# Staging copies and DMA transposes for the remainder channels of octs -1 and 0, a remainder term summed once for the two steps of a pair, and SPREAD 12, in a dilated convolution on one NeuronCore

## The chip, the cores and the metric

One core of one Trainium2 chip. The metric is the device time of one execution in microseconds (us). Runs of one kernel agree within 1%. A ratio is the mean time of one kernel's runs over that of the other's runs in the same rounds on the same chip, so it is not quite the ratio of the medians that stand beside it; its interval is a 95% interval. PE is the matrix engine, ACT the scalar engine, DVE the vector engine; SP issues the transfers.

## The reference

A causal convolution of 15 taps with dilation 2 over 16,000 steps of 144 channels, batch 2, into 288 channels; then a gate and a projection.

```python
B, T, D, K = (2, 16000, 144, 15)
xp = jnp.pad(x, ((0, 0), (28, 0), (0, 0)))
h = sum(jnp.einsum('btc,cd->btd', xp[:, 28 - 2*i : 28 - 2*i + T, :], w[i]) for i in range(K))
z = jnp.tanh(h[..., :D]) * sigmoid(h[..., D:])
return z @ w_o
```

(The loop of the reference is written as a sum here.)

## The kernel before

The time axis is cut into segments of 8 steps, "octs". A step has 144 channels, which do not fit 128 rows, so the first 128 lie transposed in `XA` and the 16 that remain are packed, several steps together, into `XBc`, and lie transposed in `XB`. The convolution runs in difference form: sums of weights (`WS`, `WC`, `WT`, `WV`, `WD`) on PE meet differences of inputs (`V`, `DU`, `DD`, `GX` to `GD`) made by DVE. The work before steady state is: octs -1 and 0 direct, as one "direct" pair and pairs 0 to 3, then "units" of two octs each, which repeat to the end. XA(3) stands for the `XA` of oct 3, and so on. `Xr` is a chunk of the input as loaded, `ZT` is `Z` transposed, `WOR` holds the weights of the projection, and a bank is one of the parts of PSUM in which PE sums.

A program in Python orders all operations by estimated times before anything runs; on the chip, each engine goes through its own list in order. So one edit can move operations far away from it. `soft` and `SPREAD` are hints to that ordering: `SPREAD` sets how early in a unit the differences of the next are put into DVE's list.

How octs -1 and 0 get their `XB` in the old kernel: 12 PE transposes into PSUM and two evictions by ACT.

```python
for o, tiles, bb in ((-1, range(E0 - 4, E0), 7), (0, range(E0, E0 + 8), 6)):
    ...
    g.add("pe", fns, r=hk5 + ["XBcz", "ID"], alloc=[bk], dur=0.06 * len(fns))
    xb_op = g.add("act", lambda v, ...: v.activation(XB[:, bslot(o), i0:8, :]..., PSb[:, ...], ACT.Copy), ...)
```

All later octs go through a staging copy `STB` (ACT or DVE) and a DMA transpose issued by SP; `XA` goes through `STA` likewise:

```python
def load_xb(o, parts=(0, 1)):
    ...
    for h in parts:
        ...   # STB[:, q, 6h:6h+6, :] <- XBc, one copy of 768 columns for each half
    return g.add("sp", lambda e: e.dma_start_transpose(XB[:, s, :, :], STB[:, q, :, :]...), ...)
```

The end of a pair adds its remainders, two matmuls for each of its two steps, and then ACT does tanh and sigmoid (`finish`) and DVE multiplies them into `Z`:

```python
def pair_end(q):
    k0 = k_of(q)
    direct_b(k0, _Half(dp[q + 1], 0))
    direct_b(k0 + 2, _Half(dp[q + 1], 1))
    return finish(dp[q + 1], zdir(k0), zdir(k0 + 2))
```

In a unit, the three combining sums of DVE (`Xp <- PS, UX`), then `PS <- PS, UX` and `PS <- PS, Xp`, give back or fill PSUM banks on which PE's next blocks (`WA,DD` and `WA,GD`) start.

Of the kernel before, what the change touches and what calls it, by code (L numbers as in the profile page):

```python
# [5 lines left out]
ACT = mybir.ActivationFunctionType  # L6
# [5 lines left out]
NP = 128  # L12
# [315 lines left out]
def _conv_wavenet_kernel(nc, x, w, w_o, out):  # L328
# [44 lines left out]
    EARLYC = 0  # L373
    NQ0 = 2
    NQD = 0
    SPREAD = 10
    SPREAS = 9
    PATTERN = "Y0a O2+ X0a+ O1+ Y0b X0b+ D11 D00 S0+ X1a+ D10 Y01 S1+ X1b+ D01 VE+ VF+ O0+"

    with contextlib.ExitStack() as st:  # L380
# [73 lines left out]
        def bslot(o):  # L454
            return (o + 1) % NB

        def oct_of(e):
            return (e - E0) // 8, (e - E0) % 8
# [5 lines left out]
        def xb_tile(e):  # L464
            o, i = oct_of(e)
            return XB[:, bslot(o), i, :]

        def win_b(e):
            c4, m4 = (e + 2) % 4, (e + 2) // 4
            return XBc[:, 4 + c4, MB - 1 - m4:MB - 1 - m4 + 8, :].rearrange("p m c -> p (m c)")  # L470
# [140 lines left out]
        g.add("pool", fix, r=xp_keys[2], w=hk, dur=0.3)  # L611
        for o, tiles, bb in ((-1, range(E0 - 4, E0), 7), (0, range(E0, E0 + 8), 6)):
            fns = []
            for e in tiles:
                c0 = bb * 1024 + 128 * oct_of(e)[1]
                fns.append(lambda t, e_=e, c=c0: t.transpose(PSb[:, c:c + 128], win_b(e_), ID[:]))
            bk = _Bank(bb)
            g.add("pe", fns, r=hk5 + ["XBcz", "ID"], alloc=[bk], dur=0.06 * len(fns))
            i0 = oct_of(tiles[0])[1]
            xb_op = g.add("act", lambda v, o=o, i0=i0, bb=bb: v.activation(XB[:, bslot(o), i0:8, :].rearrange("p a b -> p (a b)"), PSb[:, bb * 1024 + 128 * i0:bb * 1024 + 1024], ACT.Copy),  # L620
                  r=[bk], w=[("XB", bslot(o))], frees=[bk], dur=0.5 if o < 0 else 0.92)


        wak = [("WA", i) for i in range(4)]
# [40 lines left out]
        def load_xb(o, parts=(0, 1)):  # L665
            s, q = bslot(o), o % NST
            e0 = E0 + 8 * o
            ck = set()
            for e in range(e0 - 28, e0 + 8):
                if e >= EP:  # L670
                    ck.update([("XBc", chunk_of(e - E0)), ("XBd", chunk_of(e - E0))])
                else:
                    ck.update(hk5 + ["XBcz", "XBd_h"])
            m4 = (e0 + 2) // 4

            for h in parts:
                def cp(v, h=h):
                    src = bass.AP(XBc[:].tensor, (MB - 1 - m4 - h) * DB, [[8 * MB * DB, NP], [MB * DB, 6], [1, 128]])
                    dst = STB[:, q, 6 * h:6 * h + 6, :]
                    return v.tensor_copy(dst, src) if o in BDVE else v.activation(dst, src, ACT.Copy)  # L680
                g.add("dve" if o in BDVE else "act", cp, r=sorted(ck, key=str), w=[("STB", q, h)], dur=0.27 if o in BDVE else 0.708, prio=2 if gate else 0, soft=gate[:1])
            if 1 not in parts:
                return
            return g.add("sp", lambda e: e.dma_start_transpose(XB[:, s, :, :], STB[:, q, :, :].rearrange("p a b -> p (a b)")),
                  r=[("STB", q, 0), ("STB", q, 1)], w=[("XB", s)], dur=1.7, dma="xb", nbytes=12 * 128 * 128 * 2)

# [389 lines left out]

        def direct_b(k, b):
            e = H + k
            g.add("pe", region(b, [lambda: xb_tile(e), lambda: xb_tile(e - 2)], [lambda: WB[:, 0, :], lambda: WB[:, 1, :]]),
                  r=[("XB", bslot(-1)), ("XB", bslot(0)), ("WB", 0), ("WB", 1)], w=[b.bk], floating=k >= KF, prio=2 if k >= KF else 1, dur=2 * MM)  # L1080


        if ("r", 0) not in LOADS:
            load_xchunk(0).deps.add(wa_op)
# [13 lines left out]
        QS = [(0, 0), (0, 1), (1, 0), (1, 1)]  # L1098

        def jset(pi):  # L1100
            return [2 * pi, 2 * pi + 1]

        def pair_sum(q, pi, after=None):
            n, r = QS[q]
            bk = dp[q + 1]
            es = [E0 + 4 * n + r - 4 * j for j in jset(pi)]
            pre = [mm(_Half(bk, 1), lambda: ID[:], lambda: WA[:, 12, :], True)] if q == 2 and pi == 3 else []
            g.add("pe", pre + region(_Half(bk, 0), [(lambda e=e: xa_tile(e)) for e in es], [(lambda j=j: WS[:, j, :] if j < 7 else WA[:, 14, :]) for j in jset(pi)], pi == 3),
                  r=[("XA", aslot(oct_of(e)[0])) for e in es] + [("WS", pi), ("WA", pi)], dur=(2 + len(pre)) * MM, floating=True, prio=2, soft=(after,), **({"alloc": [bk]} if pi == 3 else {"w": [bk]}))
            if pi == 0:  # L1110
                g.add("act", lambda e: e.activation(bank(bk.b + 1), bank(bk.b), ACT.Copy), w=[bk], dur=t_act(N2), prio=0)  # L1111
# [13 lines left out]

        def k_of(q):
            return 2 + 4 * QS[q][0] + QS[q][1]

        def pair_end(q):
            k0 = k_of(q)  # L1130
            direct_b(k0, _Half(dp[q + 1], 0))
            direct_b(k0 + 2, _Half(dp[q + 1], 1))
            return finish(dp[q + 1], zdir(k0), zdir(k0 + 2))

        for pi, (t0, t1) in wa_order:
            for k in range(2):
                direct(k, db[k], pi, t0, t1)
            for q in range(NQ0):
                if q < NQD:
                    for i in range(2):  # L1140
                        direct(k_of(q) + 2 * i, _Half(dp[q + 1], i), pi, t0, t1)
                else:
                    pair_sum(q, pi, xb_op if q == 2 and pi == 3 else None)
        for k in range(2):
            direct_b(k, db[k])
        fin = finish(dp[0], zdir(0), zdir(1))
        for q in range(4):
            if q >= NQ0:
                for pi in range(3, -1, -1):
                    pair_sum(q, pi, (xb_op if q == 2 else fin) if pi == 3 else None)  # L1150
            for pi in range(3, -1, -1):
                if q >= NQD:
                    pair_own(q, pi)
            pair_end(q)
        load_xa(1)
        compact_chunk(0)
        g.add("act", lambda a: a.activation(WC[:, 2, 3, :], WB[:, 1, :], ACT.Copy, scale=-1.0), r=[("WB", 1)], w=[("WB", 3)], dur=0.31, prio=2)
        diff_b("dve", 3, 7, hk5 + ["XBcz"], "XBd_h")
        diff_chunk(0)
# [3 lines left out]
        for i in range(4):  # L1163
# [3 lines left out]
            else:  # L1167
                wsum(lambda: WC[:, 1, 3, :], lambda: WA[:, 12, :], lambda: WA[:, 14, :], [("WA", 3)], [("WC", 1, 3)], 0.25)
                wsum(lambda: WC[:, 0, 3, :], lambda: WC[:, 1, 3, :], lambda: WA[:, 13, :], [("WC", 1, 3), ("WA", 3)], [("WC", 0, 3)], 0.25)
        wsum(lambda: WB[:, 2, :], lambda: WB[:, 0, :], lambda: WB[:, 1, :], [("WB", 0), ("WB", 1)], [("WB", 2)], 0.25)  # L1170
        wsum(lambda: WT[:, 0:2, :], lambda: bass.AP(WC[:].tensor, 0, [[12 * N2, NP], [2 * N2, 2], [1, N2]]), lambda: bass.AP(WC[:].tensor, N2, [[12 * N2, NP], [2 * N2, 2], [1, N2]]),
# [205 lines left out]
```

## Time and profile before

| | before |
|---|---|
| median of 3 runs | 321.79 us (321.76 to 321.99) |
| profiled execution | 321.02 us, span 319.0 us, granted clock full in every stretch used here |
| matmuls | 2643 |
| busy: PE, DVE, ACT, POOL | 97%, 89%, 84%, 5% |
| DMA share of 16 engines, from 10 to 45 us | 82.6% for the hardware queue |

The prediction below shows the lines and how to read them.

### The profile page before, as it was taken

The numbers are of one execution on the slowest core, as the hardware profiler recorded it, in microseconds if no ns is written. First come the engines' busy times: TensorE is split into PE (matmuls) and PEld (weight loads), VectorE is DVE, ScalarE is ACT, GpSimd is POOL, SyncE is SP. The second block draws the span as 40 slices with busy tenths as digits, with TensorE's granted clock in tenths as the row PEclk, the third lists the DMA queues.
The fourth block names the chain that finished last, engine by engine and source line by source line (L and its number), as shares of the span: only waits on it lengthen the run. The fifth ranks groups of instructions, "written<-read, shape, count | busy, mean of one in ns | idle before, by whom it ended". The sixth has DMA issues, their size and how long they took to land.

```text
span 319.0 us, 6912 instructions
## 1 busy us (share of the span) xinstructions
PE 310.7 (97%) x2643; PEld 239.1 (75%) x2643; DVE 284.6 (89%) x615; ACT 267.5 (84%) x635; POOL 16.6 (5%) x29
## 2 busy tenths in 40 slices
PE   7999999999999999999999999999999999999994
PEld 6677667777777777777777777777777777777673
DVE  2999999999999998999989999898989989894774
ACT  3896699898897989989798897979889797788674
POOL 8106400000000000000000000000000000000000
PEclk9999999999999999999999999999999999999999
DMA  8699969949987592988949495894949477131553
GB/s 206 209 207 165 266 117 218 179 128 183 194 165 197 105 245 73 209 165 122 251 92 238 94 205 156 147 210 108 229 111 183 100 131 184 46 69 74 113 131 92
DMA packets 127821, 50.38 MB, mean 158 GB/s; under 512 B 119134, under 2 KB 121615, under 8 KB 127789
## 3 DMA queue, kind: packets, MB, share of 16 engines
q1 hardware_dynamic: 127273, 49.62, 74.1%
q0 software_dynamic: 512, 0.33, 0.4%
q8 instruction: 20, 0.33, 0.4%
q14 instruction: 12, 0.10, 0.1%
q10 hardware_dynamic: 4, 0.01, 0.0%
HBM read 11.82 MB, written 9.22 MB: 66 GB/s over the span
## 4 chain that ended last, share of the span: by engine, by line
PE 86%; ACT 7%; DMA 4%; SPq 1%; issue 1%; DVE 0%; ACTq 0%
PE PS L747 76%; PE PS L846 9%; DMA XA<-STA 2%; ACT STB L680 2%; DMA Xp<-in_x_dram 2%; ACT STA L659 1%; ACT TS L768 1%; SPq L479 1%; ACT TS L771 1%; ACT PS L905 1%; ACT XB L620 0%; SPq L491 0%; PE PS L579 0%; PE PS L877 0%; ACT XA L588 0%
## 5 line engine op out<-in xcount | busy, mean ns | idle before, releaser
L1026 DVE TENSOR_TENSOR Xp<-PS,UX 128x576 f32<-128x576 f32 x90 | 63.0, 751 | 16.7 <-PE PS L747 16.6
L747 PE MATMUL PS<-WB,XB 128*128 128x288 bf16 x260 | 72.1, 286 | 0.0
L1038 DVE TENSOR_TENSOR PS<-PS,Xp 128x576 f32<-128x576 f32 x90 | 68.4, 760 | 2.1 <-ACT OS L854 1.0
L747 PE MATMUL PS<-WA,GD 128*128 128x288 bf16 x360 | 70.0, 286 | 0.1
L768 ACT ACTIVATE TS<-PS 128x288 f16<-128x288 f32 x125 | 51.7, 413 | 13.3 <-PE PS L747 12.3
L854 ACT ACTIVATE OS<-PS 128x432 bf16<-128x432 f32 (+1 forms) x88 | 42.3, 489 | 14.0 <-PE PS L846 12.8
L771 ACT ACTIVATE TS<-PS 128x288 f16<-128x288 f32 x125 | 51.4, 411 | 0.0
L905 ACT ACTIVATE PS<-PS 128x288 f32<-128x288 f32 x120 | 46.3, 408 | 2.8 <-PE PS L747 2.8
L974 ACT ACTIVATE UX<-PS 128x576 f32<-128x576 f32 x60 | 39.2, 654 | 10.7 <-PE PS L747 10.4
L680 ACT ACTIVATE STB<-XBc 128x768 bf16<-128x768 bf16 x56 | 47.5, 854 | 0.0
L747 PE MATMUL PS<-WS,GU 128*128 128x288 bf16 x210 | 44.3, 287 | 0.0
L846 PE MATMUL PS<-WOR,ZT 128*128 128x144 bf16 (+1 forms) x322 | 42.4, 253 | 0.2 <-DVE Xp L1026 0.2
L747 PEld LDWEIGHTS PS<-WA,GD 128*128 128x128 bf16 x360 | 33.7, 98 | 11.4 <-DVE PS L1038 3.2
L776 DVE TENSOR_TENSOR Z<-TS 128x288 bf16<-128x288 f16 x125 | 36.9, 301 | 4.4 <-ACT TS L771 4.2
L747 PE MATMUL PS<-WC,XB 128*128 128x288 bf16 x120 | 34.3, 286 | 0.0
L846 PEld LDWEIGHTS PS<-WOR,ZT 128*128 128x128 bf16 x322 | 27.9, 98 | 6.6 <-ACT OS L854 0.5
L747 PE MATMUL PS<-WD,DD 128*128 128x288 bf16 x180 | 31.9, 286 | 0.2 <-ACT PS L905 0.2
L747 PE MATMUL PS<-WC,V 128*128 128x288 bf16 x180 | 30.6, 286 | 0.0
L747 PE MATMUL PS<-WA,DD 128*128 128x288 bf16 x180 | 30.6, 286 | 0.0
L747 PEld LDWEIGHTS PS<-WB,XB 128*128 128x128 bf16 x260 | 25.4, 98 | 6.7 <-ACT XB L620 0.3
L747 PE MATMUL PS<-WA,V 128*128 128x288 bf16 x118 | 25.7, 286 | 0.3 <-ACT PS L1111 0.3
L747 PE MATMUL PS<-WT,DU 128*128 128x288 bf16 x120 | 24.5, 286 | 0.0
(93 smaller groups left out, 459.4 us busy)
## 6 DMA issues: line engine op xcount, KB each, us to landing
Xr<-in_x_dram SPq DMA_DIRECT2D x15, 576.0 KB, 4.6
out_dram<-OS SPq DMA_DIRECT2D x30, 288.0 KB, 3.0
WA<-in_w_dram SPq DMA_DIRECT2D x3, 288.0 KB, 5.3
ZT<-Z SPq DMA_TRANSPOSE x32, 3.7
Xp<-in_x_dram SPq DMA_DIRECT2D x2, 252.0 KB, 5.4
XA<-STA SPq DMA_TRANSPOSE x30, 3.5
XB<-STB SPq DMA_TRANSPOSE x30, 4.4
Xp<-in_x_dram SPq DMA_DIRECT2D x1, 441.0 KB, 4.1
```

The lines of the kernel that those rows point to most:

```text
L479: return e.dma_start(tile_ap, src)
L680: return v.tensor_copy(dst, src) if o in BDVE else v.activation(dst, src, ACT.Copy)
L747: return lambda t: t.matmul(bank(bk.b), lhsT=lhs(), rhs=rhs(), start=start, stop=True, skip_group_check=True)
L768: return a.activation(TS[:, s, 0, :, :], both(bk, 0, D), ACT.Tanh)
L771: return a.activation(TS[:, s, 1, :, :], both(bk, D, D), ACT.Sigmoid)
L776: return v.tensor_tensor(dst, TS[:, s, 0, :, :], TS[:, s, 1, :, :], ALU.mult)
L846: return t.matmul(PS[:, c0:c0 + n * D], lhsT=ZT[:, zt, blk, :], rhs=WOR[:, wi:wi + n, :].rearrange("p a b -> p (a b)"), start=first, stop= ...
L854: return e.tensor_copy(dst, src) if eng == "dve" else e.activation(dst, src, ACT.Copy)
L905: g.add("act", lambda e: e.activation(bank(bk.b + 1), bank(bk.b), ACT.Copy), w=[bk], dur=t_act(N2), prio=0)
L974: g.add("act", lambda e: e.activation(UX[:, k, u % NU, :, :], both(X, 0, N2), ACT.Copy), r=[X], w=[("UX", k, u % NU)], frees=[X], dur=t_ac ...
L1026: g.add("dve", lambda v, k=k, wi=wi, vb=vb, us=us: v.tensor_tensor(wslot(wi), both(vb, 0, N2), UX[:, k, us, :, :], ALU.add), r=[vb, ("UX", ...
L1038: return v.tensor_tensor(both(d, 0, N2), src, wslot(wi), ALU.add)
```

## The change

It sends octs -1 and 0 the way of all the others: `STB`, then a DMA transpose, of 4 blocks for oct -1 and 12 for oct 0. With this the remainders of these octs are in difference form, so a term with the weights `WB0 + WB1` is common to the two steps of a pair. In pairs 2 and 3 (`SHX`) it is summed once, ahead of the copy from one bank to the other. `SPREAD` goes from 10 to 12.

```diff
+    SHX = (2, 3)
-    SPREAD = 10
+    SPREAD = 12
...
-        for o, tiles, bb in ((-1, range(E0 - 4, E0), 7), (0, range(E0, E0 + 8), 6)):
-            ... 12 PE transposes, 2 ACT evictions ...
...
+                    p0 = 2 if o < 0 else 0
+                    src = bass.AP(XBc[:].tensor, (p0 * MB + MB - 1 - m4 - h) * DB, ...)
+                    dst = STB[:, q, 6 * h + p0:6 * h + 6, :]
...
+            b0 = 8 if o < 0 else 0
+            return g.add("sp", lambda e: e.dma_start_transpose(XB[:, s, b0:12, :], STB[:, q, b0:12, :]...), ...)
...
-            region(b, [lambda: xb_tile(e), lambda: xb_tile(e - 2)], [WB0, WB1])
+            out = [(XB tile of the own difference, WB0 or -WB1)]
+            if shared_too: out.append((XB tile of the shared step, WB0 + WB1))
...
+        diff_b("dve", 1, 9, hk5 + ["XBcz"], "XBd_h")
+        load_xb(-1, (1,))
+        load_xb(0)
...
+            if pi == 0 and q in SHX:
+                tw, keys = rem(k_of(q))
+                g.add("pe", region(_Half(bk, 0), [tw[1][0]], [tw[1][1]]), ...)
...
-            direct_b(k0, _Half(dp[q + 1], 0))
-            direct_b(k0 + 2, _Half(dp[q + 1], 1))
+            direct_b(k0, _Half(dp[q + 1], 0), q not in SHX)
+            direct_b(k0 + 2, _Half(dp[q + 1], 1), q not in SHX)
...
-                    pair_sum(q, pi, xb_op if q == 2 and pi == 3 else None)
+                    pair_sum(q, pi, None)
```

(Weights and tiles are named in words where the code is long.)

More of the change, by code (lines that the diff above doesn't have):

```diff
@@ L611, in _conv_wavenet_kernel @@
         g.add("pool", fix, r=xp_keys[2], w=hk, dur=0.3)
-        for o, tiles, bb in ((-1, range(E0 - 4, E0), 7), (0, range(E0, E0 + 8), 6)):
-            fns = []
-            for e in tiles:
-                c0 = bb * 1024 + 128 * oct_of(e)[1]
-                fns.append(lambda t, e_=e, c=c0: t.transpose(PSb[:, c:c + 128], win_b(e_), ID[:]))
-            bk = _Bank(bb)
-            g.add("pe", fns, r=hk5 + ["XBcz", "ID"], alloc=[bk], dur=0.06 * len(fns))
-            i0 = oct_of(tiles[0])[1]
-            xb_op = g.add("act", lambda v, o=o, i0=i0, bb=bb: v.activation(XB[:, bslot(o), i0:8, :].rearrange("p a b -> p (a b)"), PSb[:, bb * 1024 + 128 * i0:bb * 1024 + 1024], ACT.Copy),
-                  r=[bk], w=[("XB", bslot(o))], frees=[bk], dur=0.5 if o < 0 else 0.92)
         wak = [("WA", i) for i in range(4)]
@@ L672, in load_xb @@
                 else:
-                    ck.update(hk5 + ["XBcz", "XBd_h"])
+                    ck.update(hk5 + ["XBcz", "XBd_h", "XBd0"])
             m4 = (e0 + 2) // 4
@@ L677, in cp @@
                 def cp(v, h=h):
-                    src = bass.AP(XBc[:].tensor, (MB - 1 - m4 - h) * DB, [[8 * MB * DB, NP], [MB * DB, 6], [1, 128]])
-                    dst = STB[:, q, 6 * h:6 * h + 6, :]
+                    p0 = 2 if o < 0 else 0
+                    src = bass.AP(XBc[:].tensor, (p0 * MB + MB - 1 - m4 - h) * DB, [[8 * MB * DB, NP], [MB * DB, 6 - p0], [1, 128]])
+                    dst = STB[:, q, 6 * h + p0:6 * h + 6, :]
                     return v.tensor_copy(dst, src) if o in BDVE else v.activation(dst, src, ACT.Copy)
@@ L683, in load_xb @@
                 return
-            return g.add("sp", lambda e: e.dma_start_transpose(XB[:, s, :, :], STB[:, q, :, :].rearrange("p a b -> p (a b)")),
-                  r=[("STB", q, 0), ("STB", q, 1)], w=[("XB", s)], dur=1.7, dma="xb", nbytes=12 * 128 * 128 * 2)
+            b0 = 8 if o < 0 else 0
+            return g.add("sp", lambda e: e.dma_start_transpose(XB[:, s, b0:12, :], STB[:, q, b0:12, :].rearrange("p a b -> p (a b)")),
+                  r=[("STB", q, 1)] + ([("STB", q, 0)] if o >= 0 else []), w=[("XB", s)], dur=1.7, dma="xb", nbytes=(12 - b0) * 128 * 128 * 2)
         def xbk(o):
@@ L1075, in direct, with rem, direct_b @@
                   r=[("XA", aslot(o)) for o in sorted(set(oct_of(e - DIL * i)[0] for i in range(t0, t1)))] + [("WA", pi)], dur=(t1 - t0) * MM, floating=k >= KF, prio=2 if k >= KF else 1, soft=(after,), **({"alloc": [b.bk]} if t0 == 12 and b.i == 0 else {"w": [b.bk]}))
-        def direct_b(k, b):
-            e = H + k
-            g.add("pe", region(b, [lambda: xb_tile(e), lambda: xb_tile(e - 2)], [lambda: WB[:, 0, :], lambda: WB[:, 1, :]]),
-                  r=[("XB", bslot(-1)), ("XB", bslot(0)), ("WB", 0), ("WB", 1)], w=[b.bk], floating=k >= KF, prio=2 if k >= KF else 1, dur=2 * MM)
+        def rem(k, shared_too=True):
+            o, dl = (-1, 6 + k) if k < 2 else (0, k - 2)
+            r, p = dl % 2, 3 - dl // 2
+            kk, j = p // 2, p % 2
+            bb = 6 * (1 - kk)
+            out = [(lambda: XB[:, bslot(o), bb + (2 if j == 0 else 0) + r, :], (lambda: WB[:, 0, :]) if j == 0 else (lambda: WC[:, 2, 3, :]))]
+            if shared_too:
+                out.append((lambda: XB[:, bslot(o), bb + 4 + r, :], lambda: WB[:, 2, :]))
+            return out, [("XB", bslot(o)), ("WB", 0 if j == 0 else 3), ("WB", 2)]
+        def direct_b(k, b, shared_too=True):
+            tw, keys = rem(k, shared_too)
+            g.add("pe", region(b, [x[0] for x in tw], [x[1] for x in tw]), r=keys, w=[b.bk], floating=k >= KF, prio=2 if k >= KF else 1, dur=len(tw) * MM)
+        g.add("act", lambda a: a.activation(WC[:, 2, 3, :], WB[:, 1, :], ACT.Copy, scale=-1.0), r=[("WB", 1)], w=[("WB", 3)], dur=0.31, prio=2)
+        g.add("pool", lambda p: p.tensor_copy(XBc[:, 2:4, MB - 1, :], XBc[:, 6:8, MB - 1, :]), r=hk5 + ["XBcz"], w=["XBd0"], dur=0.3)
+        diff_b("dve", 1, 9, hk5 + ["XBcz"], "XBd_h")
+        load_xb(-1, (1,))
+        load_xb(0)
+        wsum(lambda: WB[:, 2, :], lambda: WB[:, 0, :], lambda: WB[:, 1, :], [("WB", 0), ("WB", 1)], [("WB", 2)], 0.25)
         if ("r", 0) not in LOADS:
@@ L1098, in _conv_wavenet_kernel, with k_of @@
         QS = [(0, 0), (0, 1), (1, 0), (1, 1)]
+        def k_of(q):
+            return 2 + 4 * QS[q][0] + QS[q][1]
         def jset(pi):
@@ L1109, in pair_sum @@
                   r=[("XA", aslot(oct_of(e)[0])) for e in es] + [("WS", pi), ("WA", pi)], dur=(2 + len(pre)) * MM, floating=True, prio=2, soft=(after,), **({"alloc": [bk]} if pi == 3 else {"w": [bk]}))
+            if pi == 0 and q in SHX:
+                tw, keys = rem(k_of(q))
+                g.add("pe", region(_Half(bk, 0), [tw[1][0]], [tw[1][1]]), r=keys, w=[bk], dur=MM, floating=True, prio=2)
             if pi == 0:
@@ L1124, in pair_own @@
             g.add("pe", fns, r=keys, w=[bk], dur=len(fns) * MM, floating=True, prio=2)
-        def k_of(q):
-            return 2 + 4 * QS[q][0] + QS[q][1]
         def pair_end(q):
             k0 = k_of(q)
-            direct_b(k0, _Half(dp[q + 1], 0))
-            direct_b(k0 + 2, _Half(dp[q + 1], 1))
+            direct_b(k0, _Half(dp[q + 1], 0), q not in SHX)
+            direct_b(k0 + 2, _Half(dp[q + 1], 1), q not in SHX)
             return finish(dp[q + 1], zdir(k0), zdir(k0 + 2))
@@ L1149, in _conv_wavenet_kernel @@
                 for pi in range(3, -1, -1):
-                    pair_sum(q, pi, (xb_op if q == 2 else fin) if pi == 3 else None)
+                    pair_sum(q, pi, (None if q == 2 else fin) if pi == 3 else None)
             for pi in range(3, -1, -1):
@@ L1156, in _conv_wavenet_kernel @@
         compact_chunk(0)
-        g.add("act", lambda a: a.activation(WC[:, 2, 3, :], WB[:, 1, :], ACT.Copy, scale=-1.0), r=[("WB", 1)], w=[("WB", 3)], dur=0.31, prio=2)
-        diff_b("dve", 3, 7, hk5 + ["XBcz"], "XBd_h")
         diff_chunk(0)
@@ L1169, in _conv_wavenet_kernel @@
                 wsum(lambda: WC[:, 0, 3, :], lambda: WC[:, 1, 3, :], lambda: WA[:, 13, :], [("WC", 1, 3), ("WA", 3)], [("WC", 0, 3)], 0.25)
-        wsum(lambda: WB[:, 2, :], lambda: WB[:, 0, :], lambda: WB[:, 1, :], [("WB", 0), ("WB", 1)], [("WB", 2)], 0.25)
         wsum(lambda: WT[:, 0:2, :], lambda: bass.AP(WC[:].tensor, 0, [[12 * N2, NP], [2 * N2, 2], [1, N2]]), lambda: bass.AP(WC[:].tensor, N2, [[12 * N2, NP], [2 * N2, 2], [1, N2]]),
```

## The prediction

> **What bounds the kernel now.** I read the page's busy table first, then the chain that ended last, then the windows, then the timelines of PE, ACT and DVE for the first 60 us, because the change touches nothing later.
>
> ```profile
> PE 310.7 (97%) x2643; PEld 239.1 (75%) x2643; DVE 284.6 (89%) x615; ACT 267.5 (84%) x635; POOL 16.6 (5%) x29
> PE 86%; ACT 7%; DMA 4%; SPq 1%; issue 1%; DVE 0%; ACTq 0%
> 10.00:15.00 5.00, 4.58 (x52) 3.76 (x52) 4.75 (x13) 4.17 (x7) 1.24 (x3) 1.00 0.59 206
> 15.00:20.00 5.00, 5.00 (x41) 3.52 (x39) 5.00 (x17) 5.00 (x11) 0.00 (x0) 1.00 0.87 202
> 20.00:25.00 5.00, 4.67 (x39) 3.50 (x38) 4.70 (x13) 5.00 (x11) 0.00 (x0) 1.00 0.96 183
> 30.00:40.00 10.00, 9.89 (x79) 7.15 (x77) 9.86 (x22) 6.46 (x17) 5.25 (x11) 1.00 1.09 259
> 100.00:200.00 100.00, 100.00 (x843) 77.11 (x842) 93.81 (x202) 88.52 (x213) 0.00 (x0) 1.00 0.77 163
> ```
>
> PE is on 86% of the chain, and at full clock. In the windows (columns PE, PEld, DVE, ACT, POOL, clock, DMA share, GB/s) DVE idles only 0.55 us of the 15 us from 10 to 25, and ACT is full from 15 to 25: the start is a stage in which three engines are full at once. Busy PE is no measure of slack, so I summed from PE's timeline the distance of successive matmul starts. A 288-column matmul takes 0.122 to 0.123 us; at that pace all 2643 need 304.0 us, and first to last start is 313.3 us. The rest, 9.3 us, is loss: 3.1 before 10 us, 3.2 between 10 and 60, 1.3 in the middle (mostly 0.05 at a time, once per 18.75 us, DVE late), about 1.7 after 285. From 60 to 285 PE hardly waits, so a shift of PE at 60 us arrives whole at the end.
>
> **What the Trainium skill says.** "TensorE: Matmul & The Clock Gate", section Back-to-back issue gap, gives N/2.4 + 2.5 ns: 122.5 ns for N = 288; the trace's 122 to 123 ns agree, though each slice is 286 ns long. "Perfetto Trace Analysis", section Identifying the Most-Contended Engine, says matmul busy time misleads; this pair of numbers shows it. "ScalarE: Activation LUTs", section What ACT_TABLE_LOAD costs, gives 186 ns + 0.833 ns per element for an ACTIVATE with immediates and 93 ns of overlap: 826 ns for 768 columns, where the trace has 854; I use the trace and take only the slope. "Perfetto Trace Analysis", section Summary: the profiler window per engine type, says a hardware DMA's slice is its issue, not its movement; here an XB transpose issues in 1.4 to 2.4 us and lands 3.8 to 5.7 us after its start.
>
> **The change part by part.**
>
> ```profile
> 13.44 0.84 PE L616 MATMUL PS<-ID,XBc 128*128 128x128 bf16 x12
> 14.23 1.50 ACT L620 ACTIVATE XB<-PS 128x512 bf16<-128x512 bf16 x2
> 18.06 1.61 ACT L680 ACTIVATE STB<-XBc 128x768 bf16<-128x768 bf16 x2
> 22.16 1.12 ACT L659 ACTIVATE STA<-Xr 128x1024 bf16<-128x1024 bf16 x1
> 23.31 1.59 SPq L662 DMA_TRANSPOSE XA<-STA  x1
> ```
>
> PE: 12 transposes go (12 x 0.056 = 0.67 us). Of the remainder matmuls, pairs 2 and 3 sum the shared tile once, so two 288-column matmuls go (0.245 us). Sum: 0.92 us less PE work, all on the engine that sets the end. The build's order confirms 2643 to 2629 matmuls, and from matmul 261 on PE's order is the old one.
>
> ACT: the two evictions go (1.50 less an overlap of 0.1: 1.4 us). Staging copies come: one of 512 columns (854 - 256 x 0.833 = 0.64 us long, 0.53 in pace) and two of 768 (0.75 pace each): 2.0 us. ACT gains 0.6 us of work, between 13 and 25 us, where it is full. DVE: one difference of 576 for one of 448 columns, under 0.1 us. POOL: one small copy, 0.2 us, beside others. DMA and SP: two more transposes, of 4 and 12 blocks (0.5 MB), at 14 to 17 us, when SP is largely idle; before, SP has one 1.35 us transpose there. XB(0) issues at about 15.5 and, with 3.8 to 4.7 us to landing, is there by 20; PE now takes the remainders last and needs it at 20.9. That hides it.
>
> What moves matters more. The scheduler has reordered ACT, DVE and SP. In the order of the new build ACT makes the staging copies STA of octs 3 and 4 only after the tanh and sigmoid of pair 2 and all of the remainder copies; before, they run at 22.16 and 23.72. I followed the in-order engines with traced paces. PE waits for ACT's last XA eviction (13.44, as now), runs 15 matmuls, waits for the DVE sum WS at 15.7, then for the bank copy: ACT reaches it after 13.28 + 0.53 + 2 x 0.75 + 0.95 = 16.26, and it takes 0.42, so pair 0's own terms start at 16.73 (16.39 before). Seventy-three matmuls later (73 x 0.1225 = 8.94) plus 0.1 of waits, pair 2 is complete at 25.95, its last matmul's tail included. Tanh and sigmoid take ACT to 26.6, STA(3) ends at 27.65, and XA(3) is issued at 27.7 instead of 23.31.
>
> ```profile
> DMA to landing us min/median/max: 3.0/3.3/6.1
> 30.53 0.74 DVE L1026 TENSOR_TENSOR Xp<-PS,UX 128x576 f32<-128x576 f32 x1
> 33.10 0.77 DVE L1047 TENSOR_TENSOR PS<-PS,UX 128x576 f32<-128x576 f32 x1
> 33.93 0.76 DVE L700 TENSOR_TENSOR V<-XA 128x512 bf16<-128x512 bf16 x2
> 34.18 0.53 PE L747 MATMUL PS<-WA,DD 128*128 128x288 bf16 x3
> 38.46 0.42 PE L747 MATMUL PS<-WA,GD 128*128 128x288 bf16 x2
> ```
>
> The first line is the time to landing of XA transposes from 10 to 45 us; with it XA(3) lands at 30.9 to 31.2. DVE, which by my count reaches it at 30.1, must then make V(3) 0.60, DU 0.33, DD 0.61, the three L1026 sums 2.0, an L1038 0.67 and the L1047 0.77 in that order: 4.98 us, so L1047 ends at 35.9 to 36.2. Before, L1047 ended at 33.87 and PE's first block behind it (the WA,DD line) started at 34.18, unhindered. So that block starts about 1.9 us late. The present 0.26 us wait at 35.04 (for V(4), which is now behind the L1038) goes; the block at 38.46, behind V(4), DU, GX, GU, two gates and DD, I put at 40.3, again 1.85 late. In unit 1 DVE has difference work ahead of L1047 that stood behind it; PE starts there at about 45.9 against 43.8. After that PE runs without some 0.7 us of waits that the old kernel has up to 60 us (it now arrives after the engines it waited for). 2.1 - 0.7 leaves +1.4 us at 60 us, the saved matmuls already in it, since PE was counted with them.
>
> SPREAD 10 to 12 moves differences earlier in all units. In odd units DVE now does DD, gate, GV, gate, GD (1.83 us) ahead of the third L1038 instead of DD, gate, DD, gate, GV (1.96), so the 0.05 us wait per 18.75 us should go: about 12 x 0.05 = 0.6 us back. Sum: 321.8 + 1.4 - 0.6 = 322.6; I choose 322.4, because such a retuned schedule is more likely kept by its author if it helped.
>
> **The rivals.** First, the intended gain: XA(3) lands before DVE needs it or DVE's slack absorbs it; then 0.92 us of PE work and 0.4 us of the waits at 13.02 and 15.51 go, and with 0.6 us from the middle the time is 320.0 to 320.9. For it: PE is the bound over most of the span. Against it: ACT's order, and DVE without slack until 60 us. Second, DMA becomes the bound of the start: the share of the DMA is already about 1 from 20 to 40 us, the second Xr chunk is issued at about 19.6 instead of 15.76, and 0.5 MB comes on top; XB(1), XB(2) and the weights' chain behind them land 1 to 2 us later, and PE stands at the first block of unit 0. At the start's mean of about 170 GB/s 0.5 MB is 3 us of queue, of which perhaps half is hidden: 323.5 to 325. Third, it makes no difference: prologue gain and loss cancel, 321.5 to 322.
>
> **Range and chances.** The first rival sets the low end, the second the high end: 320.5 to 324.6. 2% is 6.4 us, four times any single term above, and the work that could be removed is under 1.4 us; so within 2% has 0.97, faster 0.01, slower 0.02.
>
> **What would show it.** Right: PE 2629 matmuls, 14 fewer; ACT with the XA staging copies of octs 3 and 4 after 26 us; XA(3) landing near 31; a PE wait of 1 to 2 us ahead of a WA,DD block near 34 to 36, ended by DVE L1047's successor line; no regular 0.05 us waits in the middle. Wrong: that block at 33 to 34 with no wait (then the first rival), a PE or DVE wait ended by an XB transpose before 30 us (the second), or losses from 60 to 285 us that change by more than 1 us in either direction, which would say that SPREAD and not the prologue decides.

## The result, and the profile after

The changed kernel is correct and took **322.95 us** in the median (322.29 to 323.24, 4 runs) against 321.77 us (320.89 to 321.99, 4 runs) in the same rounds: ratio **1.0039**, interval 1.0014 to 1.0064. In five further rounds on a later occasion it was 323.99 against 321.73 us (1.0052, 1.0027 to 1.0077). So the change costs about 0.4% to 0.5%, well inside "the same within 2%", although it takes work from the engine that is the bound.

First the page: the busy line and the line of the chain by engines.

```profile
PE 309.7 (97%) x2629; PEld 238.9 (75%) x2629; DVE 284.3 (89%) x615; ACT 268.1 (84%) x636; POOL 17.5 (5%) x30
PE 86%; DVE 9%; ACT 2%; DMA 1%; issue 1%; POOL 0%; ACTq 0%; POOLq 0%
```

PE has the 14 matmuls less that were predicted. On the chain DVE now has 9% where it had none (ACT has 2% where it had 7%). The windows (columns as in the prediction) tell where:

```profile
10.00:15.00 5.00, 4.87 (x47) 3.73 (x47) 4.89 (x13) 4.39 (x8) 2.07 (x4) 1.00 0.52 179
15.00:20.00 5.00, 4.69 (x38) 3.43 (x37) 5.00 (x17) 5.00 (x11) 0.00 (x0) 1.00 0.90 175
20.00:25.00 5.00, 4.82 (x40) 3.63 (x39) 5.00 (x12) 4.23 (x11) 0.00 (x0) 1.00 1.09 252
30.00:40.00 10.00, 8.26 (x62) 5.66 (x62) 9.21 (x18) 5.44 (x14) 7.06 (x14) 1.00 1.10 210
```

From 30 to 40 us PE starts 62 matmuls where the old kernel started 79. The timelines of ACT, SP, DVE and PE in that stretch, in the order of the chain (start, duration, engine, instruction; in brackets the idle time just before and what ended it):

```profile
26.46 2.00 ACT L648 ACTIVATE STA<-Xr 128x1024 bf16<-128x1024 bf16 x2
27.55 1.23 SPq L651 DMA_TRANSPOSE XA<-STA  x1
30.72 0.69 DVE L691 TENSOR_TENSOR V<-XA 128x1024 bf16<-128x1024 bf16 x1 [0.77 <-DMA XA<-STA]
32.27 2.33 DVE L1017 TENSOR_TENSOR Xp<-PS,UX 128x576 f32<-128x576 f32 x3
35.18 0.76 DVE L1038 TENSOR_TENSOR PS<-PS,UX 128x576 f32<-128x576 f32 x1
36.00 0.54 PE L738 MATMUL PS<-WA,DD 128*128 128x288 bf16 x3 [1.24 <-DVE PS L1038]
40.31 0.42 PE L738 MATMUL PS<-WA,GD 128*128 128x288 bf16 x2 [0.22 <-DVE PS L1029]
```

This is the predicted chain, link by link: STA(3) late on ACT, XA(3) late on SP, DVE idle until it lands, the sums behind it, PE standing 1.24 us. (Line numbers shift: L1038 here is the L1047 of the kernel before, L1017 its L1026, L1029 its L1038, L648 its L659.)

PE's other waits between 12.6 and 37 us, from the view of waits (line waited for, total, times, longest):

```profile
PE PS L738 <- ACT PS L896: 0.6, 2, 0.3
PE PS L738 <- DMA XB<-STB: 0.4, 1, 0.4
PE PS L738 <- DVE WS L619: 0.3, 1, 0.3
PE PS L738 <- DVE DU L691: 0.2, 1, 0.2
```

In the same stretch of the old kernel PE has one entry of this kind, 0.3 us for the ACT bank copy L1111.

**Where the time went.** Input loads before 13 us differ by up to 1.5 us from run to run, in both kernels, ahead of anything that the change touches. So I measure from the start of matmul number 110 (counted from 0), the last one before the change's first effect, to the starts of later matmuls. Number 110 is the same in both kernels; later numbers are those of the changed kernel, and the same matmuls of the old kernel are 14 further on. Profiled executions, us:

| from matmul to matmul | before | changed | difference |
|---|---|---|---|
| 110 to 260 (first pairs, start of unit 0) | 20.43 | 21.15 | +0.72 |
| 260 to 297 (rest of unit 0) | 5.14 | 6.58 | +1.44 |
| 297 to 420 (unit 1) | 15.95 | 15.82 | -0.13 |
| 420 to 2345 (the repeating middle) | 228.70 | 228.43 | -0.27 |
| 2345 to the last | 31.85 | 31.91 | +0.06 |
| 110 to the last | 302.07 | 303.89 | +1.82 |

A wait is a distance of two matmul starts beyond the pace of N/2.4 + 2.5 ns. Waits over 0.1 us between 110 and 260 sum to 0.30 + 0.16 + 0.11 + 0.50 = 1.07 us before and to 0.30 + 0.48 + 0.16 + 0.34 + 0.55 + 0.47 + 0.41 = 2.71 us after. The difference, 1.64, less the 0.92 us of work that went, is the +0.72 of the first row. In the second row stand the 1.40 us ahead of WA,DD (1.24 in the profile's own count, which ends at the modelled end of the matmul before).

### The profile page after: what moved, and what is told of

Read it like the earlier page. It is cut to its first block, busy times and chain, and to the rows that moved or that the text cites. A ratio compares the mean times of both kernels' runs of the same rounds, so it can differ in the third digit from the quotient of the medians.

```text
span 320.5 us, 6889 instructions
## 1 busy us (share of the span) xinstructions
PE 309.7 (97%) x2629; PEld 238.9 (75%) x2629; DVE 284.3 (89%) x615; ACT 268.1 (84%) x636; POOL 17.5 (5%) x30
## 4 chain that ended last, share of the span: by engine, by line
PE 86%; DVE 9%; ACT 2%; DMA 1%; issue 1%; POOL 0%; ACTq 0%; POOLq 0%
PE PS L738 74%; PE PS L837 9%; DVE V L691 1%; DVE Xp L1017 1%; DMA XA<-STA 1%; PE PS L555 1%; DVE DD L691 1%; DVE PS L1029 1%; DVE DU L691 1%; DVE GD L691 1%; DVE WC L619 1%; ACT TS L759 0%; DVE WS L619 0%; DVE Z L767 0%; ACT TS L762 0%
## 5 line engine op out<-in xcount | busy, mean ns | idle before, releaser
L1017 DVE TENSOR_TENSOR Xp<-PS,UX 128x576 f32<-128x576 f32 x90 | 63.1, 752 | 18.3 <-PE PS L738 17.9
L738 PE MATMUL PS<-WB,XB 128*128 128x288 bf16 x254 | 71.3, 286 | 0.0
L1029 DVE TENSOR_TENSOR PS<-PS,Xp 128x576 f32<-128x576 f32 x90 | 68.4, 760 | 1.8 <-ACT OS L845 1.0
L670 ACT ACTIVATE STB<-XBc 128x768 bf16<-128x768 bf16 (+1 forms) x59 | 49.6, 847 | 0.0
L738 PEld LDWEIGHTS PS<-WA,GD 128*128 128x128 bf16 x360 | 34.7, 98 | 9.8 <-DVE PS L1029 0.9
L738 PE MATMUL PS<-WC,XB 128*128 128x288 bf16 x124 | 35.5, 286 | 0.0
L738 PEld LDWEIGHTS PS<-WS,GU 128*128 128x128 bf16 x210 | 18.4, 98 | 8.8 <-ACT PS L896 1.0
```

Of the source, the lines that this page charges most:

```text
L670: return v.tensor_copy(dst, src) if o in BDVE else v.activation(dst, src, ACT.Copy)
L738: return lambda t: t.matmul(bank(bk.b), lhsT=lhs(), rhs=rhs(), start=start, stop=True, skip_group_check=True)
L1017: g.add("dve", lambda v, k=k, wi=wi, vb=vb, us=us: v.tensor_tensor(wslot(wi), both(vb, 0, N2), UX[:, k, us, :, :], ALU.add), r=[vb, ("UX", ...
L1029: return v.tensor_tensor(both(d, 0, N2), src, wslot(wi), ALU.add)
```

## The experiments

Each is an edit of one of the two kernels, mostly of the order in which operations stand in an engine's list; data and results stay the same, and all were correct. The table holds what the text then reads: time ratio to the kernel before in the same rounds, and from the profiled execution, counted from matmul 110: landing of XA(3), start of the matmul ahead of WA,DD ("PE there"), start of WA,DD, start of matmul 297 (the last WA,GD block of unit 0), and the length of the middle, 420 to 2345.

| run | ratio | XA(3) lands | PE there | WA,DD | 297 | middle |
|---|---|---|---|---|---|---|
| before | 1 | 14.52 | 21.16 | 21.29 | 25.57 | 228.70 |
| changed | 1.0039 | 18.11 | 21.89 | 23.41 | 27.73 | 228.43 |
| changed again (f0) | 1.0052 | 18.16 | 21.73 | 23.46 | 27.78 | 228.39 |
| e1 | 1.0031 | 17.63 | 21.83 | 22.92 | 27.24 | 228.43 |
| e2 | 1.0078 | 18.17 | 21.85 | 22.93 | 28.78 | 228.43 |
| e4 (old kernel) | 1.0104 | 19.17 | 23.22 | 23.34 | 29.04 | 228.70 |
| e8 (old kernel) | 1.0041 | 15.44 | 21.96 | 22.08 | 26.58 | 228.71 |
| e5 (old kernel) | 1.0010 | 14.48 | 21.16 | 22.04 | 26.08 | 228.64 |
| e6 | 1.0035 | 18.11 | 21.84 | 22.74 | 27.17 | 228.57 |
| c1 | 1.0026 | 16.34 | 21.88 | 22.95 | 27.27 | 228.42 |
| c2 | 1.0030 | 16.69 | 22.19 | 23.08 | 27.45 | 228.57 |
| f1 | 1.0154 | 20.26 | 22.15 | 25.56 | 31.21 | 228.43 |
| f2 | 1.0013 | 16.60 | 21.95 | 22.84 | 27.21 | 228.56 |
| f3 | 1.0022 | 17.15 | 22.00 | 22.88 | 27.26 | 228.57 |

How well such a stretch repeats is told by the two profiles of the same kernel:

> The changed kernel itself, as the control of the three repairs beside it, so that they are compared in the same rounds. Every theory: 1.003 to 1.005 of the kernel before, and from the matmul ahead of the first touched place (number 110) to the last matmul 303.9 us within 0.2 us, against 302.1 for the kernel before.

Up to matmul 297 they differ by 0.05 us, in the middle by 0.04; from 110 to the last they differ by 0.74 us (303.9 and 304.6), nearly all of it in one wait of unit 1, ahead of its WOR,ZT block, that was 0.89 us in one and 1.61 us in the other. That expectation (within 0.2 us) held for the parts and not for the whole. So below I use the parts; a difference under 0.1 us in them is not read, and ratios that differ by less than 0.002 are not told apart by these rounds.

### e1: the staging copy of oct 3 earlier

```diff
 # changed kernel, after the ordering
+move("act", [sta_op[3]], fin_op[2])     # STA(3) ahead of the tanh and sigmoid of pair 2
```

> The changed kernel with one instruction moved on ACT: the staging copy of oct 3 stands ahead of the tanh and sigmoid of pair 2, where ACT idles 1.63 us (24.2 to 25.9). Theory (late staging of oct 3 starves DVE, and DVE holds PE): XA(3) is issued near 26.3 instead of 27.55 and lands near 29.5; the 0.77 us that DVE idles for it at 29.9 goes, and most of the 0.38 us ahead of the gate of pair 3; the wait of PE at the first WA,DD block falls from 1.40 to about 0.4 us; the time falls by 0.7 to 1.1 us, to a ratio of 1.000 to 1.002 of the kernel before. Rival (the 0.5 MB more on the DMA queue): the wait for the XB transpose of oct 2 stays and so does the time, ratio 1.003 to 1.005.

Measured: 322.58 us against 321.42 (1.0031, 1.0008 to 1.0054). WA,DD starts 0.49 us earlier, half of what I expected. SP's timeline tells why:

```profile
25.82 1.26 SPq L822 DMA_TRANSPOSE ZT<-Z  x1
27.12 1.59 SPq L653 DMA_TRANSPOSE XA<-STA  x1
```

STA(3) was done at 25.8 us, but in SP's list the ZT transpose stands ahead of XA(3). SP was itself held up until 25.8 by the issue of XB(2), which lasted 3.26 us here, and 1.43 us in the old kernel. XA(3) therefore landed 0.48 us earlier, and WA,DD started 0.49 us earlier: what arrives early is passed on in full, but little arrived early. The chain is confirmed, the size of the remedy was wrong. The ratio alone lies in the range of the rival, and XB(2) is waited for as before; what speaks for the chain is the start of the block.

### e2: DVE's differences of oct 3 behind the combining sums

```diff
+move("dve", [v3, du3, dd3], v4)         # V, DU, DD of oct 3 behind the three combining sums
```

> The changed kernel with three instructions moved on DVE: V, DU and DD of oct 3 stand behind the third combining sum of unit 0 instead of ahead of its first. If the order on DVE were the cause, the wait at the first WA,DD block (1.40 us) goes and 1.2 us come back: ratio near 1.000. Theory (DVE is short of time in this stretch, and what counts is its idle time): the block starts near 34.8 instead of 36.0, but DVE now idles about as long ahead of the combining sums, and the wait returns at the last WA,GD block of the unit (0.39 us now, then 1.5 to 2); the time is the same within 0.3 us, ratio 1.003 to 1.005.

Measured: 324.01 us (1.0078, 1.0056 to 1.0101), slower by 1.05 us up to matmul 297. From the timelines, DVE's wait ahead of the sums and PE's two waits:

```profile
32.35 2.34 DVE L1023 TENSOR_TENSOR Xp<-PS,UX 128x576 f32<-128x576 f32 x3 [1.67 <-PE PS L744]
36.21 0.54 PE L744 MATMUL PS<-WA,DD 128*128 128x288 bf16 x3 [0.79 <-DVE PS L1044]
42.06 0.42 PE L744 MATMUL PS<-WA,GD 128*128 128x288 bf16 x2 [1.76 <-DVE PS L1035]
```

As expected, DVE now idles ahead of the sums: 1.67 us, where the differences of oct 3 had stood, because a block of PE is not ready. So WA,DD starts only 0.48 us earlier and still has a wait of 0.79 us, and the differences, now behind the sums, make the last WA,GD block wait 1.76 us where it was 0.22. That the total would stay within 0.3 us was a miss.

### e4: the same lateness put into the old kernel

```diff
 # kernel before, after the ordering
+move("act", [sta_op[3], sta_op[4]], fin_op[2], after=True)
```

> The kernel before, with the suspected cost put in alone: the staging copies of octs 3 and 4 stand on ACT behind the tanh and sigmoid of pair 2, as the new order has them; nothing else is changed. Theory: XA(3) is issued 4 us later (near 28) and lands near 31, DVE waits for it, and the old kernel loses 1 to 2 us: ratio 1.003 to 1.006. Rival (DMA load, or SPREAD): under 0.3 us, ratio 1.000 to 1.001.

Measured: 324.7 us (1.0104, 1.0073 to 1.0136), +3.5 us up to matmul 297 (29.04 against 25.57). So the move of the staging copies alone, without a new transfer or a matmul less, costs more than the whole change does (the dose is larger, too: XA(3) lands 1.06 us later than in the changed kernel). It is more than the 1 to 2 us that I expected, because the old lists are not made for it. DVE stands for XA(3), and PE in three places:

```profile
31.99 0.69 DVE L702 TENSOR_TENSOR V<-XA 128x1024 bf16<-128x1024 bf16 x1 [2.13 <-DMA XA<-STA]
```

```profile
29.90 0.30 PE L749 MATMUL PS<-WS,GU 128*128 128x288 bf16 x1 [1.12 <-ACT PS L907]
34.41 0.42 PE L749 MATMUL PS<-WT,DU 128*128 128x288 bf16 x2 [0.65 <-DVE Xp L1028]
38.79 0.42 PE L749 MATMUL PS<-WA,GD 128*128 128x288 bf16 x2 [1.52 <-DVE PS L1040]
```

Ahead of the first ACT had been busy with the two copies until 28.9 us, so that its UX and bank copies came late; the other two are V(3) late in front of the sums. The new lists spread this better: the changed kernel has 1.4 us of it and not 3.5.

### e8: the two transposes put into the old kernel

```diff
 # kernel before: two transposes of 4 and 12 blocks from WA into XB slots not yet used
+g.order["sp"].insert(g.order["sp"].index(xa_op[1]), x1)
+g.order["sp"].insert(g.order["sp"].index(xa_op[1]), x2)
```

> The kernel before, with the DMA load of the change alone: two transposes of 4 and 12 blocks from weights into two slots that are not yet used, issued ahead of the first XA transpose; nothing reads them (the slots are written again later), so the result stays right. Theory (the load is hidden): the first XA and XB transposes land up to 2 us later, the end moves by less than 0.4 us, ratio under 1.0015. Rival (DMA is the bound of the start): 1 to 2 us, ratio 1.003 to 1.006.

Measured: 322.63 us against 321.42 (1.0041, 1.0013 to 1.0069), +1.0 us up to matmul 297. My expectation was a miss: the transfers alone are not hidden in the old kernel. SP issues XA(1), and the second Xr chunk behind it, only after the two, and DVE stands for that chunk:

```profile
14.66 2.83 SPq L1311 DMA_TRANSPOSE XB<-WA  x2
17.54 1.66 SPq L664 DMA_TRANSPOSE XA<-STA  x1
23.38 0.23 DVE L546 COPY XBc<-Xr 128x256 bf16<-128x256 bf16 x1 [0.70 <-DMA Xr<-in_x_dram]
```

From matmul 110 on, XA(1) lands after 6.64 us, where it took 4.62, but no operation of DVE waits for it; the second Xr chunk lands after 8.99 us, where it took 7.03. DVE's list has the copy out of that chunk ahead of the differences of oct 1, so these come late, and PE waits for DU at 25.8 us (0.32 us). At 28.5 us PE waits another 0.47 us, ahead of a block of GU and XB. The profile names GU, but GU is done at 28.64 us and the block starts at 29.09, just after XB(2) lands at 29.00, as the changed kernel's block does (28.30 after 28.25). In the changed kernel the chunk lands later still, after 11.32 us, but the copy out of it stands late in DVE's list (26.28 us) and waits for nothing: of e8's two waits only the one for XB(2) is there. The 0.34 us for which PE waits for DU in the changed kernel have another cause, since DVE has no gap ahead of it. Whether it is SP's time for issuing the two transposes (2.83 us) or the transfers themselves that delays the chunk, e8 doesn't separate. The same ratio of e8 and of the changed kernel does not make their causes the same: e8's WA,DD block starts the moment PE is there (22.08 after 21.96), the changed kernel's 1.5 us after.

### e5 and e6: SPREAD alone

```diff
-    SPREAD = 10        # e5: the kernel before with 12
+    SPREAD = 12
```
```diff
-    SPREAD = 12        # e6: the changed kernel with 10
+    SPREAD = 10
```

> The kernel before with SPREAD 12 in place of 10 and nothing else; PE's order is unchanged, DVE's changes from unit 0 to the end. First theory (the step of the prediction): the middle of the kernel gives back 0.6 us, so the time is 0.6 us under the kernel before. Second theory (from the trace of the changed kernel, whose lag fell only from 1.7 us at 60 us to 1.5 us at 285 us): the middle gives back 0.1 to 0.3 us. Beyond both, the new order puts the DD difference of oct 3 ahead of one of the three combining sums of unit 0, which may cost up to 0.4 us there. Together I expect the kernel before, within -0.3 to +0.5 us, and a lag against the old kernel that falls by 0.1 to 0.3 us from 60 to 285 us.

> The changed kernel with SPREAD back at 10. In unit 0 DVE then does the DD difference of oct 3 behind the three combining sums and gives the WA,DD block's bank before two of the other banks. If all of the loss came from the staging copies, the WA,DD wait (1.40 us) and the time stay within 0.2 us of the changed kernel, plus 0.2 us for the middle. If SPREAD moved DVE work into the critical stretch too, the last block of unit 0 (WA,GD wait 0.39) and the WOR,ZT wait of unit 1 (0.89) shrink, the WA,DD wait may shrink by up to 0.67, and the time is 0.3 to 1.0 us under the changed kernel's. I hold the second likelier.

Measured: e5 321.79 us against 321.7 (1.0010, 0.9988 to 1.0032); e6 322.79 us (1.0035, 1.0022 to 1.0049). The ratios tell neither from its parent. The traces do. In the middle SPREAD 12 gives 0.06 us in the old kernel (228.64 against 228.70) and 0.14 us in the new one (228.43 against 228.57), not 0.6. The wait of 0.05 us once per 18.75 us did not go: with SPREAD 10 PE's starts show 0.047 and 0.035 us in turn, with SPREAD 12 about 0.035 both times. And SPREAD 12 takes time at the start: in unit 0 it puts DD(3) ahead of combining sums, so that DVE gets to the block's bank later. PE's waits for it, e5 first, then e6 (for the old kernel the block at 34.18 has none, for the changed one it is 1.24):

```profile
35.64 0.54 PE L747 MATMUL PS<-WA,DD 128*128 128x288 bf16 x3 [0.59 <-DVE PS L1047]
```

```profile
35.69 0.54 PE L738 MATMUL PS<-WA,DD 128*128 128x288 bf16 x3 [0.61 <-DVE PS L1038]
```

So SPREAD 12 costs 0.5 to 0.6 us up to matmul 297 in either kernel (26.08 against 25.57, and 27.73 against 27.17). Part of it comes back in unit 1, where old waits go (297 to 420: 15.57 us in e5 against 15.95 in the old kernel, 15.82 against 15.93 in the new one). From 110 to the last matmul SPREAD 12 costs 0.13 us net in the old kernel (302.19 against 302.06) and 0.37 in the changed one (303.89 against 303.52, one trace of each, and the whole stretch repeats less well than its parts); so of the 1.82 us of loss about 0.4 are from this one number, and about 1.45 are there with SPREAD 10, too. Of what I expected of e6, the wait ahead of WA,DD shrank, by 0.62 us; that of the last WA,GD block did not (0.39 to 0.50).

### c1 and c2: the chain repaired

```diff
 # c1: changed kernel; c2: the same with SPREAD 10
+move("act", [sta_op[3]], fin_op[2])
+move("sp", [xa_op[3]], <the ZT transpose ahead of it>)
+move("dve", [v3, du3], <the Z product and two STB copies ahead of them>)
```

> The changed kernel with the start repaired: STA(3) ahead of the tanh and sigmoid of pair 2 on ACT, XA(3) ahead of the first ZT transpose on SP, V and DU of oct 3 ahead of the Z product and of two STB copies on DVE. In e1 XA(3) still stood behind ZT and was issued only 0.43 us earlier; here it should be issued at 25.3 to 25.9 us against 27.55 and land at 28.5 to 29.3. If the chain STA(3), XA(3), V(3), combining sums is the whole cause, the WA,DD wait falls from 1.40 to 0.2 to 0.5 us and the time is 0.8 to 1.3 us under the changed kernel (equal to the kernel before, within 0.4). If the DMA load or XA(4) is the second limit, the wait goes to the last WA,GD block (XA(4) lands near 36) and only 0.2 to 0.6 us is gained.

> The same repair with SPREAD 10. If both causes are real and add, this is 0.3 to 0.8 us faster than the repaired kernel with SPREAD 12 and 0.2 to 1.0 us faster than the kernel before. If XA(4)'s landing limits both, it equals the one with SPREAD 12 within 0.3 us.

Measured: c1 322.51 us (1.0026, 1.0011 to 1.0041), c2 322.65 us (1.0030, 1.0015 to 1.0045). In c1 XA(3) lands 1.77 us earlier than in the changed kernel, and WA,DD starts only 0.46 us earlier. The next limit shows at once:

```profile
29.73 0.69 DVE L695 TENSOR_TENSOR V<-XA 128x1024 bf16<-128x1024 bf16 x1 [0.18 <-DMA XA<-STA]
32.46 2.34 DVE L1023 TENSOR_TENSOR Xp<-PS,UX 128x576 f32<-128x576 f32 x3 [0.33 <-PE PS L744]
36.33 0.54 PE L744 MATMUL PS<-WA,DD 128*128 128x288 bf16 x3 [0.79 <-DVE PS L1044]
```

Now DVE waits for PE in front of the three sums: the block whose bank they read is not finished sooner, because PE itself is late by the 0.72 us of the first row above. PE waits for DVE, which waited for PE. The same wait of DVE for PE stands ahead of the sums in e2, c2, f2 and f3, and in these five runs WA,DD starts a fixed time after PE is there, wherever XA(3) landed (16.34 to 18.17): 1.07 and 1.08 us with SPREAD 12 (c1, e2), 0.88 to 0.89 with SPREAD 10 (c2, f2, f3); e1 and e6 come within 0.02 us of it. This is the second limit. The two gains did not add in c2 (297 at 27.45, in e6 alone 27.17); its XB(2) landed 0.3 us later, and PE stood longer for it.

### f1, f2 and f3: the transfers, and everything together

```diff
 # f1: the changed kernel and this alone; f2: SPREAD 10, the moves of c1, and this
+move("sp", [xr_op[1]], <XB(0)>)          # second Xr chunk issued between XB(-1) and XB(0)
 # f3: f2, and
+move("dve", [ws_op[0]], <DD and the WB sum ahead of it>)
+move("act", [cp_op[0]], sta_op[1])        # bank copy of pair 0 ahead of STA(1)
```

> The changed kernel with the load of the second Xr chunk issued between XB(-1) and XB(0), near 15.0 us, in place of 19.6 us; nothing else. If the two added transposes and the crowd of transfers behind them are what costs the time (the DMA theory), XB(1) and XB(2) land 0.5 to 1.5 us earlier, the 0.55 us wait of PE for XB(2) at 27.6 us goes, and the time falls by 0.5 to 1.0 us. If the chain STA(3), XA(3), V(3), combining sums sets the WA,DD block (the first theory), the XB(2) wait goes all the same, but the WA,DD block starts no earlier, its wait grows by what PE gained, and the time stays within 0.25 us of the changed kernel. I hold the second likelier.

Measured: 327.18 us against 321.73 (1.0154, 1.0124 to 1.0185), against 1.0052 for the changed kernel beside it. Neither theory had expected a loss of 3.2 us, and not all of it is the chain: behind the 3.12 us wait shown below PE runs at a granted clock of 0.5 from 39.28 to 42.69 us (0.62 on average from 38.3 to 42.5 in the windows), and 13 matmuls in a row start 0.24 us apart instead of 0.12. From WA,DD to 297 it takes 5.65 us, where the changed kernel takes 4.32; so 1.33 of the 3.48 us lost up to 297 are the clock's. All six runs of f1 have a lower mean clock (0.987 to 0.995) than those of f0 (0.997 to 0.999), so its ratio is not used below. XB(2) did not land earlier (15.75 us after matmul 110 against 15.66); XB(0) landed 1.8 us later, ACT waited 0.35 us for it, and XA(3) was issued 0.56 us later and took 4.74 us to land, where it had taken 3.15:

```profile
28.32 1.24 SPq L653 DMA_TRANSPOSE XA<-STA  x1
33.09 0.69 DVE L693 TENSOR_TENSOR V<-XA 128x1024 bf16<-128x1024 bf16 x1 [2.30 <-DMA XA<-STA]
38.37 0.54 PE L740 MATMUL PS<-WA,DD 128*128 128x288 bf16 x3 [3.12 <-DVE PS L1040]
```

By accident this is the cleanest test of the chain. XA(3) lands 2.15 us later than in the changed kernel, and WA,DD starts 2.15 us later. In all four runs with these DVE lists it starts the same time after the landing: 5.30 us in both profiles of the changed kernel, 5.29 in e1, 5.30 in f1, over a spread of 2.6 us. Both points lie ahead of the slow clock. Why XA(3) took 1.6 us longer on its way I can't settle from one profile; the crowd in the queues is a guess.

> SPREAD 10, the earlier STA(3), XA(3), V(3) and DU(3), and the earlier Xr load together. If the chain and the DMA each hid the other's gain, both go at once: the WA,DD wait falls under 0.5 us, the XB(2) wait is gone, and from matmul 110 to the end it takes 302.3 to 303.0 us, 0.9 to 1.6 us less than the changed kernel. If PE's own waits for ACT ahead of WA,DD (0.47 and 0.41 us) and the three sums that need PE's blocks are a third limit of the same length, it stays at 303.2 to 303.6 us.

Measured: 322.53 us (1.0013, 0.9991 to 1.0035), 0.4% under the changed kernel in the same rounds. It is the lowest ratio of my versions of the changed kernel, but c1 and f3 are within 0.002 of it, and from 110 to the last matmul e1 is even shorter (303.40 us against 303.63); it is not to be told from the kernel before. Here XB(2) lands 1.1 us earlier and PE's wait for it is gone, but 297 stays at 27.21 (27.17 with SPREAD 10 alone): PE loses at other places what it does not lose there. Its waits of 0.2 us and more from 23 to 37 us:

```profile
23.76 0.42 PE L744 MATMUL PS<-WT,DU 128*128 128x288 bf16 x2 [0.56 <-DVE DU L695]
30.36 0.30 PE L744 MATMUL PS<-WS,GU 128*128 128x288 bf16 x1 [0.31 <-ACT PS L902]
33.48 0.66 PE L744 MATMUL PS<-WD,DD 128*128 128x288 bf16 x4 [0.24 <-ACT PS L902]
35.48 0.54 PE L744 MATMUL PS<-WA,DD 128*128 128x288 bf16 x3 [0.60 <-DVE PS L1044]
```

The expectation of 302.3 to 303.0 us from matmul 110 to the last was missed; the rival, a third limit (303.2 to 303.6), came out at 303.63.

> As the one before, and at 14 us DVE makes the last WS sum ahead of a DD difference and of the WB sum, and ACT makes the bank copy of pair 0 ahead of STA(1). PE's waits at 14.9 us (0.48) and 16.1 us (0.16) should go. If PE's early arrival is passed on, the stretch from matmul 110 to the end is 0.3 to 0.6 us shorter than without it, and the kernel reaches the kernel before within 0.4 us; if a transfer or DVE takes it back by 30 us, there is no difference over 0.15 us.

Measured: 322.66 us (1.0022, 0.9999 to 1.0045), 297 at 27.26. The wait for WS at 14.9 us is gone (that for the bank copy, 0.16, stays), and PE waits 0.85 us for XB(0) at 20.5 us in its place, where f2 waits 0.25: a transfer took it back, as the second half of the expectation had it.

What I couldn't try: in the old kernel PE does 12 matmuls of pair 3's own terms between the blocks of unit 0, where the changed kernel waits 0.47 and 0.41 us for ACT; there they cover the same latency. In the changed kernel they are all done before. Moving them back ended in a deadlock of the lists when I built it, since the bank of pair 3 is already given to a later copy of ACT; such a kernel can't be run. So that these waits are the uncovered side of that order is argued from the two timelines, not shown by a run.

## Why the prediction was right or wrong

The time (322.4 predicted, 322.95 measured, range 320.5 to 324.6), its direction and its main path were right. The size of the change was not: +0.6 us was forecast, and +1.2 was measured by the medians (+2.3 in the later rounds; by the ratios +1.3 and +1.7). That the two times agree within 0.2% says little, since any change of this size is small beside 320 us; and the step from 322.6 down to 322.4 rested on a guess about the author and led away from the result. Most steps can be laid beside the trace.

- **Less PE work**: 2643 to 2629 matmuls and the issue at full pace 0.92 us less. Right (304.0 to 303.08 us).
- **ACT's copies**: the three STB copies at 12.97 us take 2.09 us busy; the sum 0.53 + 2 x 0.75 said 2.03. Right.
- **Pairs**: pair 0's own terms 16.36 us (said 16.73), tanh of pair 2 at 25.87 (25.95), STA(3) done at about 27.5 (27.65), XA(3) issued 27.55 (27.7) and landed 30.70 (30.9 to 31.2). Right, and a little early throughout since matmul 110 started 0.3 us earlier than in the old kernel's profile.
- **The new wait**: WA,DD at 36.00 us (35.9 to 36.2), ended by the successor of L1047, and the last WA,GD block at 40.31 (40.3). Right, with a little luck: counted from matmul 110 both are 0.3 us later than these clock times say, just outside the forecast. e4 shows that the copies' place alone makes such a loss, f1 and e1 that the block follows XA(3)'s landing one for one.
- **Unit 1**: said 2.1 us late, measured 2.35 at the WOR,ZT block and 2.21 at the WA,DD block that was meant; +1.4 at 60 us, measured +1.7 (2.0 if counted from matmul 110). The term that was mis-sized is the 0.7 us of old waits that were to go behind that block: 0.48 went, the two waits of 0.12 and 0.35 us in unit 1. Ahead of it the wait for WOR,ZT even grew, from 0.39 to 0.89 us.
- **XB(0) hidden**: right, PE has no wait for it in the changed kernel. But the second rival, the DMA, was held for too small. Its sign, a PE wait ended by an XB transpose before 30 us, is there (0.4 us in the view of waits). XB(1) and XB(2) land 2.1 us later, counted from matmul 110, than in the old kernel, as that rival had it. e8 shows that the two transposes alone cost the old kernel 1.0 us, in part by a wait for the second Xr chunk that the changed kernel doesn't have, in part by one for XB(2) that it has. This wait, 0.55 us by the distance of starts, is part of why PE is late at WA,DD; how much the time would fall without it is not shown, since in f2, where it is gone, PE waits as long elsewhere and arrives no earlier.
- **The step that failed is SPREAD**: "about 12 x 0.05 = 0.6 us back". The middle gave 0.27 us, of which SPREAD has 0.14 (e6; 0.06 in the old kernel, e5). The small wait that was to go shrank from 0.047 to 0.035 us, eleven times or so, and there was a second one of 0.035 that I had not counted; so the step was right in sign and four times too large. I had also counted nothing against it at the start, where it costs 0.5 us up to the end of unit 0; over the whole kernel it costs 0.1 to 0.4 us and gives nothing (e5, e6). The argument that an author keeps such a number because it helps was worth nothing here.
- **What I did not see**: most of PE's waits before matmul 260, 1.64 us more than in the old kernel. Those for WS and the bank copy (0.64 us) were in my count, and 0.1 us of the rest; not in it were 0.34 us for DU (but for that 0.1), 0.55 for XB(2) and 0.47 and 0.41 for ACT. It did little harm to the number, since WA,DD was later still; it is why no repair of the chain (c1, f2) gets back more than about half a microsecond.

Where the expected gain went, then: 0.92 us of PE work is taken away and spent on waits in the same stretch, 1.64 us of them, before the bank of unit 0's WA,DD block is waited for another 1.4 us. Two limits of nearly the same length stand behind each other, and removing one shows the other: with the chain repaired (f2) matmul 297 is still 1.64 us later than in the old kernel, 0.79 since PE is there later and 0.76 since PE, once there, waits 0.89 us for the sums and not 0.13.

## What to carry to other kernels

Work taken from the bound engine is worth nothing until the last arrival at its next wait comes earlier; so follow the chain to that arrival, and after it name the second one, for it caps every repair. When a program orders the lists, read the new order and not the diff: here a moved staging copy cost more than the saved work gave, and one spreading number added to it; both were outside the part that the change was about. Compare stretches from a common matmul rather than whole times when the start varies by more than the effect.

## What the Trainium skill lacked or had wrong

- "TensorE: Matmul & The Clock Gate", section Back-to-back issue gap, calls N/2.4 + 2.5 ns an isolated gap that under-counts at small N and gives about 81 ns for N = 128 in a stream of weight load and matmul pairs. In these runs pairs of weight load and 288-column matmul keep 122 to 123 ns, which is that formula, over the whole kernel (but for the stretch of half clock in f1); and the 12 PE transposes of 128 columns in the old kernel, each with its weight load, start 56 ns apart, the formula's 55.8 ns, not 81.
- "Perfetto Trace Analysis", section Summary: the profiler window per engine type, counts a lock wait into the slice of a hardware DMA, without a size. Here the slice is no constant: the XB(2) transpose is issued in 1.43 us in the old kernel, in 3.13 and 3.26 us in the changed kernel and e1, and in 2.02 us in f1; it then holds up what stands behind it in the list, ZT and XA(3) in e1. That it is the lock that makes the difference is not shown.
- No page I read gives the time from issue to landing of a transpose beside other transfers: XA transposes of one size took 3.0 to 6.1 us in the old kernel from 10 to 45 us, and XA(3) took 3.15 us in the changed kernel and 4.74 in f1.
